# Drawing the waits on two PSUM tensors by bank instead of by tensor

## The chip, the cores and the metric

The kernel runs on one core of a Trainium2 chip. The metric is the device time of one execution in microseconds (us). The core has five engines that run their own instruction streams and meet through semaphores: PE (TensorE, matrix products), DVE (VectorE), ACT (ScalarE), POOL (GpSimd) and SP (here the queue that issues most DMAs). PE writes its products into PSUM, a memory of eight banks; DVE and ACT read them from there.

## The reference, cut to what matters

```python
# q, k, v: 8 batches x 8 heads x 576 positions x 64
scores = q @ k.T / 8                       # heads 0-3: the last 32 positions;
attn = softmax(where(mask, scores, -1e9))  # heads 4-7: same position modulo 32, not later
x = (attn @ v)                             # as 4608 tokens x 512
h = x @ w_in                               # 4608 x 1024
e = exp(h - max(h)); sm = e / (sum(e) + 1e-9)
solu = h * sm
ln = (solu - mean(solu)) / sqrt(var(solu) + 1e-6) * g_ln
out = ln @ w_out                           # 4608 x 512
```

## The kernel before

The work has two halves that run side by side. The attention is cut into 40 units, five for each of the 8 batches. A unit's scores are made by PE in the PSUM tensor `s_ps` (L445 puts the mask in, L450 adds the products). DVE takes the maxima (L456) and subtracts them (L457), ACT takes the exponential (L459), DVE, POOL and ACT normalise it, a DMA turns it (`pt`, L480), and PE multiplies it by v into `x_ps` (L502). ACT (L518) and DVE (L519) copy the result as a high and a low f16 part into `xhi` and `xlo`.

The feed-forward part is cut into 36 tiles of 128 tokens, numbered 0 to 35 here; function `ff(n, ...)` writes tile n. For one tile:

1. PE makes the first product (`x @ w_in`) into two banks of `h_ps`, in two halves of 512 columns. A half is 12 products of 512 columns (L560, L561, L562 in turn).
2. DVE takes the negated maximum of both halves (L567) and prepares scales (L568, L574, L575).
3. ACT takes the exponential out of `h_ps` (L578, into `eu`; each such instruction is followed by a short row that reads the accumulated sum).
4. DVE multiplies `h_ps` by that exponential (L581, into `eu` too) and makes a mean (L584). It is the last reader of the tile's two banks.
5. ACT and DVE make the f16 parts `c` (L585, L586), ACT the squares (L588), POOL the norm's factor (L592 to L596), and a DMA turns `c` into `ct` (L599).
6. PE makes the second product (L604, L605, L606) into `o_ps`, also in two halves of 12. ACT scales it (L612) and issues the store (L613).

The PSUM tensors are `s_ps` (2 banks), `h_ps` (3), `x_ps` (2) and `o_ps` (1). In the last tiles (34 and 35) the second product goes to `s_ps`, and tile 35's first product to `x_ps`. A tile's first product uses two of the three banks of `h_ps`: banks 0 and 1, then 0 and 2, then 1 and 2, in a cycle of three tiles; the half that is made first goes to the bank that the tile just before does not use.

Class `Plan` collects all steps (`add`) with an engine, an estimated time, a key, and what each step reads and writes, by bank for `h_ps` and `x_ps` (names such as `("h", 1)`, `("x", 0)`). `order` makes one list of all steps from the keys and these dependencies, and the kernel then calls every step's function in that order. Each engine executes its instructions in that order, one after the other. The waits between engines are not drawn from the plan: the layer under the kernel draws them while the instructions are recorded, from the tensors that each instruction reads and writes. For a PSUM tensor it puts an access of one engine behind the accesses of other engines that were recorded before it, whichever bank of the tensor they touch. If the plan's list has the first half of tile n+1 ahead of the exponential of tile n, that exponential therefore waits for that half, although it lies in another bank.

A per-batch scale is also made: ACT sums squares of v (L378), DVE adds two of them up (L325), PE spreads the sum over the partitions (L332, into `s_ps`), and DVE makes the scale (L336 to L342). w_out is prepared early, by ACT and DVE (L629 to L631, L685, L686).

Of the kernel before, what the change touches and what calls it, by code (L numbers as in the profile page):

```python
# [86 lines left out]
]  # L87


class Plan:  # L90

# [6 lines left out]
    SKIP = {"act": 0.1, "dve": 0.08, "pe": 0.07, "pool": -0.1}  # L98

    def __init__(self):  # L100
        self.steps = []
        self.writer, self.readers = {}, {}

    def add(self, eng, dur, fn, key, r=(), w=(), lock=None, dma=None, after=()):

        n = len(self.steps)
        deps = set(after)
        for x in r:
            if x in self.writer:
                deps.add(self.writer[x])  # L110
        for x in w:
            if x in self.writer:
                deps.add(self.writer[x])
            deps.update(self.readers.get(x, ()))
        for x in r:
            self.readers.setdefault(x, []).append(n)
        for x in w:
            self.writer[x], self.readers[x] = n, []
        deps.discard(n)
        lock = eng == "pool" if lock is None else lock  # L120
        self.steps.append((eng, dur, fn, key, deps, lock, dma))
        return n

    def order(self):
        steps = self.steps
        left = [len(s[4]) for s in steps]
        users = [[] for _ in steps]
        for n, s in enumerate(steps):
            for d in s[4]:
                users[d].append(n)  # L130
        ready_at = [0.0] * len(steps)
        free = dict.fromkeys(("pe", "act", "dve", "pool", "sp"), 0.85)
        locked = dict.fromkeys(("dve", "pool"), 0.0)
        dma_free, moved, pieces = 3.0, 0, []
        waiting = {e: [] for e in free}
        for n, s in enumerate(steps):
            if not left[n]:
                waiting[s[0]].append(n)
        out = []
        while len(out) < len(steps):  # L140
            best = None
            for e, ns in waiting.items():
                if not ns:
                    continue
                now = max(free[e], min(ready_at[n] for n in ns))
                n = min((n for n in ns if ready_at[n] <= now), key=lambda n: (steps[n][3], n))
                if best is None or now < best[0]:
                    best = now, e, n
            now, e, n = best
            waiting[e].remove(n)  # L150
            out.append(n)
            dur = steps[n][1]
            if e == "sp":
                pushes, issue, begins, lands = steps[n][6]
                start = max(now + begins, dma_free)
                dma_free = start + dur
                pieces.append((start, dma_free, moved, moved + pushes))
                moved += pushes
                free[e] = now + issue + 0.06
                for a, b, c, d in reversed(pieces):  # L160
                    if c < moved - self.DEEP <= d:
                        free[e] = max(free[e], a + (b - a) * (moved - self.DEEP - c) / (d - c))
                        break
                end = dma_free + lands + (LATE0 if steps[n][6] == LOAD and now < 20 else self.LATE)
            else:
                if steps[n][5]:
                    now = max(now, locked["pool" if e == "dve" else "dve"])
                    locked[e] = now + dur
                end = now + dur
                free[e] = end - (0.16 if dur > 2.4 else self.SKIP[e])  # L170
            for m in users[n]:
                left[m] -= 1
                ready_at[m] = max(ready_at[m], end + (0.0 if steps[m][0] == e else self.HOP))
                if not left[m]:
                    waiting[steps[m][0]].append(m)
        self.span = max(free.values())
        return out


@with_exitstack  # L180
def attn_solu_kernel(ctx: ExitStack, tc: tile.TileContext, qloc, qstr, kloc, kstr, vloc, vstr, w_in, w_out, g, masks, out):
    nc = tc.nc
# [63 lines left out]
    h_ps = ps.tile([P, 3, 512], F32, name="h_ps")  # L246
    x_ps = ps.tile([P, 2, 512], F32, name="x_ps")
    o_ps = ps.tile([P, DM], F32, name="o_ps")

    plan = Plan()  # L250
# [3 lines left out]
    def init():  # L254
        for i, x in enumerate((-0.5, DEEP * P_SCALE / TOP, P_SCALE)):
            nc.gpsimd.memset(consts[:, i : i + 1], x)
        for x in vsc_sb:
            nc.gpsimd.memset(x[:, 3:4], 1.0 / TOP)
            nc.gpsimd.memset(x[:, 4:5], -1.0 / TOP)

    add("pool", 1.2, init, -9, w=["consts"])
    add("dve", 0.3, lambda: nc.vector.memset(ones, 1.0), -9, w=["ones"])

    def masks_bf16():
# [6 lines left out]
    def load_masks(key):  # L271
        add("sp", 0.4, lambda: nc.sync.dma_start(mask_sb, masks), key, w=["mask_raw"], dma=LOAD)
        add("dve", 1.0, masks_bf16, key, r=["mask_raw"], w=["mask"])
# [248 lines left out]

    def ff(n, key, key2):

        banks, halves = (((0, 1), (0, 1)), ((0, 2), (1, 0)), ((1, 2), (0, 1)))[n % 3]
        hv, o, O = h_ps[:, banks[0] : banks[1] + 1 : banks[1] - banks[0]], o_ps, "o"
        HH = [("h", i) for i in banks]

        if n >= NT - 2:
            o, O = s_ps[:, n % 2], ("s", n % 2)  # L530
        if n == NT - 1:
            hv, HH = x_ps, [("x", i) for i in range(2)]
# [7 lines left out]
        nm, up, down, low, z, us, mean, sq, near, ia, zb, zc, v, r, f = (st[:, i : i + 1] for i in range(15))  # L540
# [23 lines left out]
        for i in halves:  # L564
# [4 lines left out]
            r=[(ST, "low"), *SC, "consts"], w=[(ST, "nm")])  # L569

        def span():
# [7 lines left out]
            r=[*HH, (ST, "nm"), *SC], w=[E, (ST, "z")])  # L579

        add("dve", 1.3, lambda: nc.vector.scalar_tensor_tensor(uv, hv, ia, ev, op0=ALU.mult, op1=ALU.mult, accum_out=us), key + 0.3,  # L581
            r=[*HH, E, (ST, "ia")], w=[U, (ST, "us")])
# [4 lines left out]
            r=[U, (ST, "mean"), (C, 0)], w=[(C, 1)], lock=True)  # L587
        add("act", 1.24, lambda: nc.scalar.activation(junk[:, 0:DF], u, AF.Square, bias=mean, scale=1.0, accum_out=sq), key + 0.42,  # L588
            r=[U, (ST, "mean")], w=["junk", (ST, "sq")])
# [109 lines left out]
    for b in range(B):  # L699
        if b:  # L700
            load_qk(b, 1, LK[b])
        v_split(b, 1, VK[b] + 0.5)
        for j in range(2):
            unit(b * NU + j, UK[b * NU + j], PK[b * NU + j])
        if b:
            load_qk(b, 0, LK[b] + 2)
        v_split(b, 0, VK[b] + 2.5)
        for j in range(2, NU - 1):
            unit(b * NU + j, UK[b * NU + j], PK[b * NU + j])
        if b + 1 < B:  # L710
            if b == 0:
                prep_o()
            load_v(b + 1, 1, LK[b + 1] + 0.5)
            load_v(b + 1, 0, LK[b + 1] + 2.5)
            v_scale(b + 1, VK[b + 1])
        unit(b * NU + NU - 1, UK[b * NU + NU - 1], PK[b * NU + NU - 1])
        if b == 0:
            split_o()
        while t < NT and (t * P + P - 1) // S <= b:
            ff(t, TK[t], GK[t])  # L720
            t += 1

    for n in plan.order():
        plan.steps[n][2]()


# [59 lines left out]
```

## Time and profile before

| | before |
|---|---|
| median of 3 runs | 530.99 us (529.46 to 534.56) |
| the profiled execution | 528.67 us, of it a span of 527.0 us from the first to the last instruction |
| mean granted TensorE clock | 0.974 |
| PE busy | 476.0 us (90%) |
| DVE busy | 359.3 us (68%) |
| ACT busy | 294.3 us (56%) |
| POOL busy | 153.8 us (29%) |

In a view of groups or of waits a row names the engine, the tensor written and the line. "A <- B: 5.7, 7, 1.4" says that A's engine sat idle before it for 5.7 us in total, in 7 waits of which the longest was 1.4 us, and that B ended those waits. In a timeline a row is: start, duration, engine, line, operation, out<-in with shapes, how many in a row, and in brackets the idle time of the engine just before it with what ended it. A step that waited although its engine was busy with nothing shows this idle time; products of 512 columns start about 0.22 us apart and have rows of 0.38 us, since they overlap in the array.

### The profile page before, as it was taken

The numbers are of one execution on the slowest core, as the hardware profiler recorded it, in microseconds if no ns is written. First come the engines' busy times: TensorE is split into PE (matmuls) and PEld (weight loads), VectorE is DVE, ScalarE is ACT, GpSimd is POOL, SyncE is SP. The second block draws the span as 40 slices with busy tenths as digits, with TensorE's granted clock in tenths as the row PEclk, the third lists the DMA queues.
The fourth block names the chain that finished last, engine by engine and source line by source line (L and its number), as shares of the span: only waits on it lengthen the run. The fifth ranks groups of instructions, "written<-read, shape, count | busy, mean of one in ns | idle before, by whom it ended". The sixth has DMA issues, their size and how long they took to land.

```text
span 527.0 us, 11895 instructions
## 1 busy us (share of the span) xinstructions
PE 476.0 (90%) x4858; PEld 246.1 (47%) x4858; DVE 359.3 (68%) x679; ACT 294.3 (56%) x414; POOL 153.8 (29%) x258
## 2 busy tenths in 40 slices
PE   1547969989999999989999899999998999989996
PEld 1434534444544555445544455545543545444442
DVE  3597978577964888477954878577963789743540
ACT  1689966574736555645646456735655546433441
POOL 4342562423421233223331242212331223211120
PEclk9857998999999999999999999999999999999999
DMA  8999998449996799839995499989973597723351
GB/s 231 406 320 267 313 262 177 91 106 223 243 207 131 165 241 227 176 95 194 309 182 108 117 202 298 196 201 228 221 132 69 144 199 143 121 62 82 78 107 54
DMA packets 168294, 96.51 MB, mean 183 GB/s; under 512 B 138032, under 2 KB 154800, under 8 KB 167728
## 3 DMA queue, kind: packets, MB, share of 16 engines
q1 hardware_dynamic: 163056, 86.32, 75.3%
q10 hardware_dynamic: 5184, 9.44, 5.6%
q8 instruction: 38, 0.62, 0.5%
q14 instruction: 16, 0.13, 0.1%
HBM read 40.03 MB, written 9.44 MB: 94 GB/s over the span
## 4 chain that ended last, share of the span: by engine, by line
PE 74%; DVE 12%; DMA 5%; issue 4%; ACT 3%; POOL 1%; SPq 0%; ACTq 0%; DVEq 0%; POOLq 0%
PE h_ps L560 12%; PE h_ps L562 11%; PE h_ps L561 11%; PE o_ps L604 9%; PE o_ps L605 8%; PE o_ps L606 8%; PE s_ps L450 4%; PE x_ps L502 4%; DVE st L567 3%; DVE eu L581 3%; DMA vtwo<-vstr 2%; DMA pt<-p 2%; PE s_ps L445 1%; PE h_ps L656 1%; DMA ct<-c 1%
## 5 line engine op out<-in xcount | busy, mean ns | idle before, releaser
L560 PE MATMUL h_ps<-w,xhi 128*128 128x512 f16 x280 | 107.0, 382 | 8.8 <-DVE eu L581 5.7
L561 PE MATMUL h_ps<-w,xhi 128*128 128x512 f16 x280 | 106.9, 382 | 0.0
L562 PE MATMUL h_ps<-w,xlo 128*128 128x512 f16 x280 | 106.7, 381 | 0.1
L604 PE MATMUL o_ps<-obuf,ct 128*128 128x512 f16 x272 | 103.4, 380 | 0.9 <-ACT ob L612 0.8
L606 PE MATMUL o_ps<-obuf,ct 128*128 128x512 f16 x272 | 103.1, 379 | 0.0
L605 PE MATMUL o_ps<-obuf,ct 128*128 128x512 f16 x272 | 103.1, 379 | 0.0
L468 POOL TENSOR_TENSOR t<-t,m 128x576 f32<-128x576 f32 (+2 forms) x40 | 52.3, 1309 | 135.8 <-DVE m L465 106.1
L581 DVE SCALAR_TENSOR_TENSOR eu<-h_ps,st,eu 128x1024 f32<-128x1024 f32 x35 | 44.8, 1280 | 40.7 <-PE h_ps L562 19.2
L567 DVE TENSOR_REDUCE st<-h_ps 128x1 f32<-128x1024 f32 x35 | 42.6, 1218 | 42.3 <-PE h_ps L562 42.0
L585 ACT ACTIVATE c<-eu,st 128x1024 f16<-128x1024 f32 x36 | 41.3, 1147 | 41.2 <-DVE st L584 39.5
L578 ACT ACTIVATE eu<-h_ps,st,vsc 128x1024 f32<-128x1024 f32 x31 | 37.3, 1204 | 47.8 <-DVE st L568 22.1
L586 DVE SCALAR_TENSOR_TENSOR c<-eu,st,c 128x1024 f16<-128x1024 f32 x36 | 45.9, 1276 | 22.1 <-ACT c L585 22.1
L594 POOL TENSOR_SCALAR st<-st 128x1 f32<-128x1 f32 x36 | 23.5, 653 | 120.9 <-ACT junk L588 120.0
L561 PEld LDWEIGHTS <-xhi 128*128 128x128 f16 x288 | 28.3, 98 | 41.0 <-issue 11.2
L459 ACT ACTIVATE t<-t 128x576 f32<-128x576 f32 (+2 forms) x40 | 27.5, 686 | 33.9 <-DVE t L457 32.6
L562 PEld LDWEIGHTS <-xlo 128*128 128x128 f16 x288 | 28.3, 98 | 34.9 <-issue 0.8
L604 PEld LDWEIGHTS <-ct 128*128 128x128 f16 x288 | 28.1, 97 | 34.7 <-issue 3.1
L606 PEld LDWEIGHTS <-ct 128*128 128x128 f16 x288 | 28.2, 98 | 34.0
L560 PEld LDWEIGHTS <-xhi 128*128 128x128 f16 x288 | 28.3, 98 | 32.7 <-issue 0.8
L450 PE MATMUL s_ps<-k,q 64*54 64x54 f32 (+1 forms) x1280 | 41.1, 270 | 2.7 <-DMA k<-kstr 1.8
L605 PEld LDWEIGHTS <-ct 128*128 128x128 f16 x288 | 28.2, 98 | 31.7 <-issue 2.2
L450 PEld LDWEIGHTS s_ps<-k,q 64*54 64x54 f32 (+1 forms) x1280 | 39.5, 198 | 3.3 <-issue 3.3
(148 smaller groups left out, 704.9 us busy)
## 6 DMA issues: line engine op xcount, KB each, us to landing
out<-ob ACTq DMA_DIRECT2D x36, 256.0 KB, 3.3
vtwo<-vstr SPq DMA_DIRECT2D x9, 768.0 KB, 7.2
vd<-vtwo SPq DMA_DIRECT2D x14, 384.0 KB, 9.0
vrl<-vloc SPq DMA_DIRECT2D x8, 640.0 KB, 5.7
q<-qstr SPq DMA_DIRECT2D x8, 594.0 KB, 4.9
k<-kstr SPq DMA_DIRECT2D x8, 594.0 KB, 5.6
q<-qloc SPq DMA_DIRECT2D x8, 576.0 KB, 4.5
k<-kloc SPq DMA_DIRECT2D x8, 576.0 KB, 6.8
```

The costliest lines, as they stand in the source:

```text
L450: nc.tensor.matmul(s_ps[row : row + nq, pair, i * nk : (i + 1) * nk], q_raw[half][hs, q0 : q0 + (nq - 1) * nqb + 1 : nqb], k_raw[half][hs, ...
L468: add("pool", nx * nk / 510 + 0.02, lambda: nc.gpsimd.tensor_tensor(tv, tv, sm.unsqueeze(2).broadcast_to([P, nx, nk]), op=ALU.mult), key + ...
L560: nc.tensor.matmul(hv[:, i], xhi[:, cc, tok], whi[:, cc, cols], start=(cc == 0), stop=False)
L561: nc.tensor.matmul(hv[:, i], xhi[:, cc, tok], wlo[:, cc, cols], start=False, stop=False)
L562: nc.tensor.matmul(hv[:, i], xlo[:, cc, tok], whi[:, cc, cols], start=False, stop=(cc == 3))
L567: add("dve", 1.21, lambda: nc.vector.tensor_reduce(low, hv, axis=AX.XY, op=ALU.max, negate=True), key + 0.2, r=HH, w=[(ST, "low")])
L581: add("dve", 1.3, lambda: nc.vector.scalar_tensor_tensor(uv, hv, ia, ev, op0=ALU.mult, op1=ALU.mult, accum_out=us), key + 0.3, r=[*HH, E, ...
L585: add("act", 1.2, lambda: nc.scalar.activation(c[:, 0], u, AF.Identity, bias=mean, scale=1.0), key + 0.35, r=[U, (ST, "mean")], w=[(C, 0)])
L586: add("dve", 1.28, lambda: nc.vector.scalar_tensor_tensor(c[:, 1], u, mean, c[:, 0], op0=ALU.add, op1=ALU.subtract), key + 0.4, r=[U, (ST, ...
L604: nc.tensor.matmul(o, ct[:, cc, :], ohi[:, cc, :], start=(cc == 0), stop=False)
L605: nc.tensor.matmul(o, ct[:, cc, :], olo[:, cc, :], start=False, stop=False)
L606: nc.tensor.matmul(o, ct[:, 8 + cc, :], ohi[:, cc, :], start=False, stop=(cc == 7))
```

## The change

A step's PSUM waits on `h_ps` and `x_ps` are taken out of the hands of the layer below and drawn from the plan's dependencies. `Plan.add` notes for each PE, ACT and DVE step which of the two tensors it touches. A new function `emit` replaces the loop that called the steps. After a step is recorded, it declares that its instructions do not depend on another engine's earlier accesses to the same tensor, except on those of the steps that the plan names; and it adds, for each of these, a wait of the step's first instruction for the last instruction of the named step. On PE a step's first instruction is a weight load, so a wait that stood at the product can now stand at the weight load ahead of it.

The banks of a tile change too: even tiles use banks 0 and 1, odd tiles banks 1 and 2, and odd tiles make their second half of columns first. So the first half made goes to bank 0 or 2, which the tile before last used, and the second half made always goes to bank 1, which the tile just before uses.

```diff
+BANKED = ("h", "x")
...
     def add(self, eng, dur, fn, key, r=(), w=(), lock=None, dma=None, after=()):
...
+        self.spaces.append({x[0] for x in (*r, *w) if isinstance(x, tuple) and x[0] in BANKED} if eng in ("pe", "act", "dve") else set())
         self.steps.append((eng, dur, fn, key, deps, lock, dma))
...
+def emit(nc, tc, plan):
+    same_bank = mybir.DependencyInfo(mybir.DependencyClass.Sync, mybir.DependencyReason.DATA)
+    made = {}
+    for n in plan.order():
+        eng = plan.steps[n][0]
+        k = len(nc.cur_bb.bb.instructions)
+        plan.steps[n][2]()
+        if not plan.spaces[n]:
+            continue
+        made[n] = new = list(nc.cur_bb.bb.instructions[k:])
+        for x in sorted(plan.spaces[n]):
+            true = [d for d in sorted(plan.steps[n][4]) if x in plan.spaces[d] and plan.steps[d][0] != eng]
+            for i in new:
+                for other in ("pe", "act", "dve"):
+                    if other != eng:
+                        tc.declare_no_dep(i, group=x + other, keep=[j for d in true for j in made[d]], reason="another bank")
+            for d in true:
+                tc.add_manual_dep(new[0], made[d][-1].name, same_bank, reason="the same bank")
+        for x in sorted(plan.spaces[n]):
+            for i in new:
+                tc.add_to_no_dep_group(x + eng, i)
...
     def ff(n, key, key2):
-        banks, halves = (((0, 1), (0, 1)), ((0, 2), (1, 0)), ((1, 2), (0, 1)))[n % 3]
-        hv, o, O = h_ps[:, banks[0] : banks[1] + 1 : banks[1] - banks[0]], o_ps, "o"
+        banks, halves = (((0, 1), (0, 1)), ((1, 2), (1, 0)))[n % 2]
+        hv, o, O = h_ps[:, banks[0] : banks[1] + 1], o_ps, "o"
...
-    for n in plan.order():
-        plan.steps[n][2]()
+    emit(nc, tc, plan)
```

The new function pushes the lines below it down by 28, so that the first product stands at L588 to L590 after the change. No instruction changes its place on any engine: all five lists are the same, line numbers apart. What moves are the waits. In the rows below the names in brackets are the semaphores for which an instruction waits, each named after the engine that raises it.

The first place is on PE, where the first half of tile 28's first product (into `h_ps`, from `xhi` and `xlo`) follows the end of a second product (`o_ps`). Before:

```order
L606 LDWEIGHTS ct_107
L606 MATMUL o_ps<-obuf_121,ct_107 128x512
L560 LDWEIGHTS xhi_101 [waits Activation_49]
L560 MATMUL h_ps<-w_120,xhi_101 128x512 [waits Activation_49]
L561 LDWEIGHTS xhi_101
L561 MATMUL h_ps<-w_120,xhi_101 128x512
```

After:

```order
L634 LDWEIGHTS ct_107
L634 MATMUL o_ps<-obuf_121,ct_107 128x512
L588 LDWEIGHTS xhi_101 [waits Activation_49]
L588 MATMUL h_ps<-w_120,xhi_101 128x512
L589 LDWEIGHTS xhi_101
L589 MATMUL h_ps<-w_120,xhi_101 128x512
```

The wait at the product, which was for tile 27's exponential (L578 on ACT), is gone; the wait at the weight load, for the copy into `xhi` (L518), stays.

The second place is on DVE, from the maximum of tile 31 (L567, `st_115`) to the start of tile 32's. Before:

```order
L567 TENSOR_REDUCE st_115<-h_ps 128x1 [waits PE_49]
L568 TENSOR_TENSOR st_115<-st_115 128x3 [waits DVE_49]
L574 TENSOR_SCALAR st_115<-st_115 128x1 [waits DVE_49]
L575 TENSOR_SCALAR st_115<-st_115 128x1 [waits DVE_49]
L581 SCALAR_TENSOR_TENSOR eu_104,st_115<-h_ps,st_115,eu_104 128x1024 [waits DVE_49,PE_49,Activation_49]
L584 TENSOR_SCALAR st_115<-st_115 128x1 [waits DVE_49]
```

After:

```order
L595 TENSOR_REDUCE st_115<-h_ps 128x1 [waits PE_49]
L596 TENSOR_TENSOR st_115<-st_115 128x3 [waits DVE_49]
L602 TENSOR_SCALAR st_115<-st_115 128x1 [waits DVE_49]
L603 TENSOR_SCALAR st_115<-st_115 128x1 [waits DVE_49]
L609 SCALAR_TENSOR_TENSOR eu_104,st_115<-h_ps,st_115,eu_104 128x1024 [waits DVE_49,Activation_49]
L612 TENSOR_SCALAR st_115<-st_115 128x1 [waits DVE_49]
```

The multiplication of tile 31 (L581) no longer waits for PE: that wait was for the first half of tile 32. In many other places, such as the maxima (L567) of tiles 13 and 18, the brackets read the same before and after, but the count that is waited for is lower: it was that of the next tile's first half, which is recorded earlier, and is now that of the tile's own second half.

Of the 72 halves, 22 have a wait at the first weight load before and 44 after; the first product itself has one in 44 before and in none after.

More of the change, by code (lines that the diff above doesn't have):

```diff
@@ L100, in __init__ @@
     def __init__(self):
-        self.steps = []
+        self.steps, self.spaces = [], []
         self.writer, self.readers = {}, {}
```

## The prediction

> **What bounds the kernel now.** I read the page first, for the engine that is never free.
>
> ```profile
> span 527.0 us, 11895 instructions
> PE 476.0 (90%) x4858; PEld 246.1 (47%) x4858; DVE 359.3 (68%) x679; ACT 294.3 (56%) x414; POOL 153.8 (29%) x258
> PE   1547969989999999989999899999998999989996
> L560 PE MATMUL h_ps<-w,xhi 128*128 128x512 f16 x280 | 107.0, 382 | 8.8 <-DVE eu L581 5.7
> ```
>
> PE is busy for 476.0 of 527.0 us. So a wait is worth what it leaves PE idle, and no more: 51 us in all. The row of 40 slices (13.2 us each, busy tenths) shows where: much of it lies in the first four slices, where the weights are prepared, and from the seventh on PE is at 8 or 9 tenths until the last. The view of waits says which can be touched by this change.
>
> ```profile
> DVE eu L581 <- PE h_ps L562: 19.2, 6, 4.7
> ACT eu L578 <- PE h_ps L562: 14.1, 5, 4.1
> PE s_ps L445 <- DVE t L457: 5.9, 3, 5.0
> PE h_ps L560 <- DVE eu L581: 5.7, 7, 1.4
> PE s_ps L332 <- DVE vs L325: 4.4, 4, 1.5
> PE x_ps L502 <- DVE xlo L519: 3.2, 1, 3.2
> PE h_ps L560 <- ACT eu L578: 1.9, 2, 1.6
> PE h_ps L560 <- DVE st L567: 0.8, 2, 0.4
> ```
>
> The first two rows are DVE and ACT waiting, for 33.3 us, for a first product that is not their own tile's (their own is done when L567 has read it). DVE and ACT have time to spare, so these 33 us count only where PE then waits for DVE or ACT. That is what the six rows of PE show.
>
> **The change part by part.** No instruction is added, removed or moved, so the sum is one of PE's idle times that go.
>
> *First halves that wait for another bank.* Tile 28's is the largest.
>
> ```profile
> 405.36 1.18 ACT L578 ACTIVATE eu<-h_ps,st,vsc 128x1024 f32<-128x1024 f32 x1
> 406.69 0.38 PE L560 MATMUL h_ps<-w,xhi 128*128 128x512 f16 x1 [1.58 <-ACT eu L578]
> 406.90 0.38 PE L561 MATMUL h_ps<-w,xhi 128*128 128x512 f16 x1
> ```
>
> PE sits idle for 1.58 us until tile 27's exponential (406.54) and its read-out are over. That exponential reads banks 0 and 1; the half goes to bank 2. The order's rows show that the wait goes. Its bank's last reader, by the new numbering bank 0, was tile 26.
>
> *Second halves that wait for a late multiplication.* The second half shares its bank with the tile just before, before and after the change, and must wait for that tile's L581. But L581 was itself held.
>
> ```profile
> 466.08 0.19 ACT L578 ACTIVATION_READ_ACCUMULATOR eu<-h_ps,st 128x1 f32 x1
> 470.06 1.28 DVE L581 SCALAR_TENSOR_TENSOR eu<-h_ps,st,eu 128x1024 f32<-128x1024 f32 x1 [4.68 <-PE h_ps L562]
> 471.41 0.38 PE L560 MATMUL h_ps<-w,xhi 128*128 128x512 f16 x1 [1.44 <-DVE eu L581]
> ```
>
> Tile 31's exponential is there at 466.27. DVE idles 4.68 us until PE has finished tile 32's first half (just under 470), multiplies until 471.4, and PE idles 1.44 us for it. With the false wait gone the multiplication ends near 467.7, before PE asks.
>
> Not every such wait is false. At 68.45 DVE comes to L581 without any idle time (its row has no bracket), so this wait stays:
>
> ```profile
> 67.11 1.28 DVE L581 SCALAR_TENSOR_TENSOR eu<-h_ps,st,eu 128x1024 f32<-128x1024 f32 x1
> 68.45 0.38 PE L560 MATMUL h_ps<-w,xhi 128*128 128x512 f16 x1 [1.23 <-DVE eu L581]
> 79.92 0.56 PE L560 MATMUL h_ps<-w,xhi 128*128 128x512 f16 x1 [0.21 <-DVE eu L581]
> ```
>
> I keep 68.45 and 79.92 (1.4 us). The three rows of L560 add up to 5.7 + 1.9 + 0.8 = 8.4 us, so **7.0 us** go, in 9 waits.
>
> *The scale of v, L332.* L325 stands behind a maximum (L567) on DVE, and that maximum waits for the next tile's first half.
>
> ```profile
> 223.98 0.38 PE L562 MATMUL h_ps<-w,xlo 128*128 128x512 f16 x1
> 223.99 0.19 ACT L378 ACTIVATION_READ_ACCUMULATOR junk<-vtwo 128x1 f32 x1
> 226.98 1.23 DVE L567 TENSOR_REDUCE st<-h_ps 128x1 f32<-128x1024 f32 x1 [6.58 <-PE h_ps L562]
> 228.32 0.16 PE L332 MATMUL s_ps<-vs,ones 128*128 128x1 bf16 x1 [1.38 <-DVE vs L325]
> 341.10 0.16 PE L332 MATMUL s_ps<-vs,ones 128*128 128x1 bf16 x1 [0.22 <-DVE vs L325]
> ```
>
> Tile 13's product ends with the row at 223.98 (224.4), its maximum starts 2.6 us later, and L325's other input is ready at 224.18. Started at 224.4, the maximum and L325 are done before 226; PE asks at 226.9. Of the 4.4 us in four waits, the one at 341.10 (0.22 us) has no such maximum ahead of it and stays; the other two are built like this one: **4.2 us** go.
>
> *The copies of x, L502 at 78.72.* Here too a maximum holds DVE.
>
> ```profile
> 70.82 0.38 PE L562 MATMUL h_ps<-w,xlo 128*128 128x512 f16 x1
> 74.62 1.23 DVE L567 TENSOR_REDUCE st<-h_ps 128x1 f32<-128x1024 f32 x1 [2.40 <-PE h_ps L562]
> 78.12 0.55 DVE L519 TENSOR_TENSOR xlo<-x_ps,xhi 128x384 f16<-128x384 f32 x1
> 78.72 0.99 PE L502 MATMUL x_ps<-pt,vd 118*64 118x54 f16 x48 [3.22 <-DVE xlo L519]
> ```
>
> DVE's 2.40 us go (it waits for tile 2's first half; its own product was done at 71.2, with the row at 70.82), everything between on DVE follows, and PE's 3.22 us shrink by **2.4 us**.
>
> *The clock behind that wait.* Two windows after it (PE's busy time and count come first, the granted clock third from the end):
>
> ```profile
> 79.90:83.50 3.60, 3.58 (x9) 1.31 (x9) 3.60 (x7) 3.52 (x6) 0.00 (x0) 0.53 0.92 181
> 83.50:87.00 3.50, 3.50 (x18) 1.56 (x16) 3.50 (x5) 2.09 (x4) 1.23 (x1) 1.00 1.10 248
> ```
>
> After 3.22 us idle the granted clock is 0.53 for 3.6 us: 9 products where the next 3.5 us hold 18. That costs half of it, 1.8 us. A wait of 1.58 us (tile 28's) was followed by products at full distance, 0.21 us. With 0.8 us left at this place I expect no dip: **1.8 us**; the other end is 0, if the dip stays. The Trainium skill ("TensorE: Matmul & The Clock Gate", Part 1) says that the clock halves after an idle window of about 3.4 us, which runs freely. The trace agrees in size (0.53, 3.6 us). By that rule the dip's going would be likely and not certain, and the sum would stay within these two ends.
>
> *The mask's product, L445.* Of the three waits for L457 (5.9 us) the longest, 5.0 us, is in the preparation; the other two, 0.9 us, come late, the first of them here:
>
> ```profile
> 422.60 1.28 DVE L581 SCALAR_TENSOR_TENSOR eu<-h_ps,st,eu 128x1024 f32<-128x1024 f32 x1 [2.70 <-PE h_ps L562]
> 425.56 0.31 PE L445 MATMUL s_ps<-mk_str,unit 64*64 64x270 bf16 x4 [0.48 <-DVE t L457]
> ```
>
> DVE comes to these L457 without idle time after a false wait of 2.70 us: **0.9 us** go.
>
> *What the idle figures leave out.* The rows at 406.69 and 406.90 start 0.21 us apart but last 0.38, so a stall behind a 512-column product is longer than its idle figure by 0.17 us. Nine of the waits above stand behind such a product: **1.5 us**.
>
> *The waits that move to the weight load.* These could cost. A half's weights take 98 ns to load, and 44 halves now carry a wait there, 22 more than before. Exposed each time that is 22 x 0.1 = 2.2 us; where the wait is long satisfied it may be nothing. Tile 7's first half has its wait at the weight load already:
>
> ```profile
> L560 PEld LDWEIGHTS <-xhi 128*128 128x128 f16 x288 | 28.3, 98 | 32.7 <-issue 0.8
> 142.57 0.38 PE L606 MATMUL o_ps<-obuf,ct 128*128 128x512 f16 x1
> 142.79 0.38 PE L560 MATMUL h_ps<-w,xhi 128*128 128x512 f16 x1
> ```
>
> It starts 0.22 us after the product ahead, the full rate. I take 0, and keep 2.2 for the range. The Trainium skill (same page, Part 2, step 1) says that PE pulls weight loads ahead of products in flight. That speaks against the change, since a load that waits can't be pulled ahead; by it the sum would be 15.6 us. The row above shows no such loss.
>
> **Sum:** 7.0 + 4.2 + 2.4 + 1.8 + 0.9 + 1.5 = 17.8 us.
>
> *What is late next.* PE then reaches its other waits earlier. One is already tight:
>
> ```profile
> 92.22 1.28 DVE L581 SCALAR_TENSOR_TENSOR eu<-h_ps,st,eu 128x1024 f32<-128x1024 f32 x1 [0.48 <-ACT eu L578]
> 93.60 0.39 PE L560 MATMUL h_ps<-w,xhi 128*128 128x512 f16 x1
> 75.00:100.00 25.00, 21.57 (x222) 10.65 (x215) 21.70 (x41) 15.50 (x24) 10.41 (x14) 0.93 0.74 166
> ```
>
> L581 ended at 93.5. Mostly these follow PE's own earlier work and move with it; where DVE has little room (21.70 of 25 us here) they do not. Between nothing and all given back, I am nearer to nothing, because every DVE and ACT wait that goes lets them run ahead as well: 3.8 us, a fifth. **Net 14.0 us.** The profiled execution took 528.67 us, 1.67 around its span, and would take 514.7. The median of the runs is 530.99, 2.3 above it; taken off that, **517.0 us**.
>
> The last stretch does not help or hurt: PE's waits there are for ACT's L612 reading `o_ps` and `s_ps`, which the change leaves alone.
>
> **The rivals.**
>
> *Next waits take the place* (most of the gain is lost). If DVE's dense stretches, 25 to 100 us, and the attention's waits (L445 for L457) bind, PE's removed idle time comes back as another. For it: the tight wait at 93.60. Against it: DVE is 68% busy, and some 33 us of its and ACT's own waiting go. What surely stays are the direct first halves, 1.9 + 0.8 = 2.7 us, and about half of the rest: (17.8 - 2.7) / 2 + 2.7 would be 10; at a quarter it is 6.5 us, so 524.5 us.
>
> *The change doesn't do what it says.* Where the layer below still orders `h_ps` by tensor through another semaphore, the time stays at 531. Against it are the order's rows at tiles 28 and 31.
>
> *Slower, by DMAs that land later.* All turned tiles go through one queue. If the earlier starts of `ct` and `pt` fall together with loads, each lands later, and PE meets it. None of PE's waits above ended on a DMA, so the room is unknown. To eat up 17.8 us, the 36 `ct` would have to reach PE 0.5 us late each; at 0.7 us the kernel is at 538. Nothing points to it: a transfer that starts earlier has as much longer to land.
>
> **How the numbers follow.** Forecast (10 to 18 us gained, 513 to 521): 0.62. More than that, since ACT and DVE may also hurry the early stretch: 0.05. The next waits: 0.25, centred at 524.5, of which 0.18 lies below 525.7. Without effect: 0.05. Slower: 0.03. Faster by over 1% (below 525.7; 1% is about what a measurement of this kernel can tell from no change) is then 0.62 + 0.05 + 0.18 = 0.85; within 1% 0.07 + 0.05 = 0.12; slower 0.03. The range leaves out 2 in 10: from 511.5 (all of the sum and 1.7 us more) to 525, which takes in the dip of the clock, the 2.2 us of weight loads and most of the first rival.
>
> **What the profile will show.** Right: the rows of DVE's and ACT's waits for `h_ps` products of another tile (19.2 and 14.1 us) are gone or small; L588's idle time (now 8.8) falls to about 2; the four waits of L332 keep under 1 us; the granted clock has no dip near 78 us; PE's busy time hardly changes, since the rows are the same. Wrong would be: L588's idle time at 8 again, L473 or L530 (the mask's and x's products) with several us of new idle time, or products spaced wider than 0.22 us.

## The result and the profile after

The changed kernel takes 514.18 us (median, 512.16 to 520.89) against 530.23 us (529.14 to 534.56) of the kernel before in the same session: a ratio of 0.967, 95% interval 0.959 to 0.975. The forecast was 517.0 us with a range of 511.5 to 525. An execution over 1.5% above the fastest of its kernel is not in a ratio: 520.89 us here, and in the second measurement of the changed kernel further down 526.30 and 702.49 us of its six (and 821.70 us of the kernel before).

The profiled execution took 512.16 us, of it a span of 510.4: 16.6 us less than the span before. First the page: the span, the engines, PE's row of slices, and three groups.

```profile
span 510.4 us, 11874 instructions
PE 474.6 (93%) x4858; PEld 246.3 (48%) x4858; DVE 360.0 (71%) x679; ACT 296.0 (58%) x414; POOL 154.6 (30%) x258
PE   1548989999999999999999999999999999999996
L588 PE MATMUL h_ps<-w,xhi 128*128 128x512 f16 x280 | 107.2, 383 | 1.5 <-DVE eu L609 1.4
L606 ACT ACTIVATE eu<-h_ps,st,vsc 128x1024 f32<-128x1024 f32 x31 | 37.3, 1203 | 33.8 <-DVE st L596 33.4
L609 DVE SCALAR_TENSOR_TENSOR eu<-h_ps,st,eu 128x1024 f32<-128x1024 f32 x35 | 44.7, 1277 | 8.2 <-ACT eu L606 7.9
```

PE does the same work (474.6 us busy against 476.0), and from the seventh slice on every slice but the last stands at 9. L588's idle time fell from 8.8 to 1.5 us. The exponential and the multiplication now wait for what they use, and no longer for PE: the view of waits has no row any more in which one of them waits for a product. Of its rows these bear on the forecast:

```profile
DVE st L595 <- PE h_ps L590: 43.5, 23, 4.2
PE s_ps L473 <- DVE t L485: 5.0, 1, 5.0
PE x_ps L530 <- DMA pt<-p: 2.6, 2, 1.5
PE h_ps L588 <- DVE eu L609: 1.4, 2, 1.2
PE s_ps L360 <- DVE vs L353: 0.2, 1, 0.2
```

The first row is DVE's wait for its own tile (42.0 us before, when some of it was for the next tile's half: the longest was 6.8 us, now 4.2). Of the waits of PE that the sum named, the two that were to stay stayed (L588, 1.2 and 0.2 us), and so did the one in the preparation (L473, 5.0). One row is longer than before: the transposed weights of the attention, `pt` (1.9 us in one wait before, now two).

Four places of the timeline, in time order:

```profile
152.10 0.82 PE L530 MATMUL x_ps<-pt,vd 118*64 118x54 f16 x40 [1.16 <-DMA pt<-p]
393.72 1.20 ACT L606 ACTIVATE eu<-h_ps,st,vsc 128x1024 f32<-128x1024 f32 x1 [0.86 <-DVE st L596]
394.60 0.38 PE L588 MATMUL h_ps<-w,xhi 128*128 128x512 f16 x1
455.35 0.38 PE L588 MATMUL h_ps<-w,xhi 128*128 128x512 f16 x1
```

Tile 28's first half starts at 394.60 without idle time, while tile 27's exponential is still running (393.72 to 394.92): they are on different banks, and that is the change at work. Tile 31's second half (455.35) finds its bank free. The row at 152.10 is the one new wait.

### The profile page after: what moved, and what is told of

Same layout as the page of the kernel before. It is cut to its first block, busy times and chain, and to the rows that moved or that the text cites. A ratio compares the mean times of both kernels' runs of the same rounds, so it can differ in the third digit from the quotient of the medians.

```text
span 510.4 us, 11874 instructions
## 1 busy us (share of the span) xinstructions
PE 474.6 (93%) x4858; PEld 246.3 (48%) x4858; DVE 360.0 (71%) x679; ACT 296.0 (58%) x414; POOL 154.6 (30%) x258
## 4 chain that ended last, share of the span: by engine, by line
PE 81%; DMA 6%; DVE 5%; ACT 2%; issue 2%; SPq 2%; POOL 1%; ACTq 0%; POOLq 0%
PE h_ps L588 11%; PE h_ps L589 11%; PE h_ps L590 11%; PE o_ps L632 11%; PE o_ps L634 10%; PE o_ps L633 10%; PE s_ps L478 6%; PE x_ps L530 5%; DMA k<-kloc 4%; DMA pt<-p 3%; PE s_ps L473 2%; DVE obuf L714 1%; PE h_ps L684 1%; DVE eu L609 1%; SPq L448 1%
## 5 line engine op out<-in xcount | busy, mean ns | idle before, releaser
L588 PE MATMUL h_ps<-w,xhi 128*128 128x512 f16 x280 | 107.2, 383 | 1.5 <-DVE eu L609 1.4
L590 PE MATMUL h_ps<-w,xlo 128*128 128x512 f16 x280 | 106.7, 381 | 0.0
L632 PE MATMUL o_ps<-obuf,ct 128*128 128x512 f16 x272 | 103.4, 380 | 0.9 <-ACT ob L640 0.8
L595 DVE TENSOR_REDUCE st<-h_ps 128x1 f32<-128x1024 f32 x35 | 42.7, 1220 | 43.5 <-PE h_ps L590 43.5
L622 POOL TENSOR_SCALAR st<-st 128x1 f32<-128x1 f32 x36 | 21.4, 595 | 108.6 <-ACT junk L616 107.6
L546 ACT CAST xhi<-x_ps 128x384 f16<-128x384 f32 (+2 forms) x40 | 21.7, 547 | 41.5 <-PE x_ps L530 36.6
L484 DVE TENSOR_REDUCE m<-s_ps 128x6 f32<-128x576 f32 (+2 forms) x40 | 30.4, 760 | 21.2 <-PE s_ps L478 21.2
L590 PEld LDWEIGHTS <-xlo 128*128 128x128 f16 x288 | 28.4, 98 | 34.4 <-issue 0.8
L588 PEld LDWEIGHTS <-xhi 128*128 128x128 f16 x288 | 28.2, 98 | 34.5 <-DVE eu L609 1.9
L632 PEld LDWEIGHTS <-ct 128*128 128x128 f16 x288 | 28.1, 98 | 31.7
```

Of the source, the lines that this page charges most:

```text
L588: nc.tensor.matmul(hv[:, i], xhi[:, cc, tok], whi[:, cc, cols], start=(cc == 0), stop=False)
L590: nc.tensor.matmul(hv[:, i], xlo[:, cc, tok], whi[:, cc, cols], start=False, stop=(cc == 3))
L595: add("dve", 1.21, lambda: nc.vector.tensor_reduce(low, hv, axis=AX.XY, op=ALU.max, negate=True), key + 0.2, r=HH, w=[(ST, "low")])
L632: nc.tensor.matmul(o, ct[:, cc, :], ohi[:, cc, :], start=(cc == 0), stop=False)
```

## Where the 16.5 us came from

PE's instruction list is the same, so the same half of a first product can be looked up in both timelines, and the difference of its starts is the time gained so far:

| start before | start after | gained | what lies between this row and the one above |
|---|---|---|---|
| 53.31 | 53.15 | 0.16 | the preparation |
| 71.82 | 73.36 | -1.54 | after: the clock is halved from 68.9 to 72.3 |
| 79.92 | 78.39 | 1.53 | the wait of L502 at 78.72 |
| 84.19 | 80.99 | 3.20 | before: the clock is halved from 80.0 to 83.4 |
| 115.37 | 110.52 | 4.85 | L332's first wait (1.5), a short one of L560 (0.3), less 0.15 at the tight place (93.60 before, 90.55 after) |
| 154.91 | 148.18 | 6.73 | three waits of L560 |
| 164.47 | 158.98 | 5.49 | after: the wait for `pt` at 152.10 |
| 232.72 | 225.23 | 7.49 | a wait of L560, L332's second wait |
| 296.15 | 287.10 | 9.05 | L332's third wait |
| 399.77 | 389.40 | 10.36 | two waits of L560 (1.1), a short one inside a half (0.3) |
| 406.69 | 394.60 | 12.09 | tile 28's first half (1.58 + 0.17) |
| 430.97 | 417.65 | 13.32 | the two late waits of L445 (1.0), a short one of L560 (0.1) |
| 458.08 | 443.63 | 14.46 | L560 |
| 471.41 | 455.35 | 16.06 | tile 31's wait (1.44 + 0.17) |
| 477.06 | 460.53 | 16.53 | the last wait of L560 |

It stays at 16.53 to the last first product. Added up by kind, as the sum of the prediction has them (its 1.5 us for what the idle rows leave out is shared among the nine waits that it was for: five of L560, two of L332, two of L445):

| | forecast | found |
|---|---|---|
| L560's waits | 7.0 + 0.9 | 8.8 |
| L332 | 4.2 + 0.3 | 4.6 |
| L502 | 2.4 | 3.1 |
| L445 | 0.9 + 0.3 | 1.0 |
| smaller steps | - | 0.4 |
| the clock | 1.8 | 0.0 |
| what is late next | -3.8 | -1.4 |
| net | 14.0 | 16.5 |

## The experiments

All kernels below are the changed kernel with the edit shown; none changes the work of PE, DVE or ACT, and where the output changes it is said. Ratios are to the kernel before on the same chip.

**Which part of the change?** The first edit keeps the new banks and leaves all waits to the layer below:

```diff
-BANKED = ("h", "x")
+BANKED = ()
```

> The new banks of the tiles alone, with all waits drawn by tensor as before. Theory (the gain is the removed waits, and the renumbering of banks only makes them removable): the time of the kernel before, ratio 1.00, about 530 us, with PE's 8.4 us of idle time ahead of L588 back. Rival (contiguous banks let the layer below tell banks apart by itself): 514 to 518 us, and PE's idle time ahead of L588 under 3 us.

Measured: 531.38 us, 0.997 (0.994 to 1.001). The waits are those of before, to the tenth:

```profile
DVE eu L609 <- PE h_ps L590: 19.2, 6, 4.7
ACT eu L606 <- PE h_ps L590: 14.1, 5, 4.1
PE h_ps L588 <- DVE eu L609: 5.7, 7, 1.4
```

The two-tile alternation of banks is worth nothing by itself. The other half of that question, waits by bank with the old cycle of three, was not tried: a tile on banks 0 and 2 is read by one access that steps over bank 1, while PE may be writing there. The next two name one tensor each:

```diff
-BANKED = ("h", "x")
+BANKED = ("h",)
```

> Waits by bank for h_ps alone, x_ps by tensor. Theory (nearly all of it comes from h_ps; of the waits named in the prediction none was a false one on x_ps): 514 to 516 us, ratio 0.970. Rival (the copies L546 and L547, freed of each other, carry much of it): 519 us or more, ratio 0.98 or above.

Measured: 514.31 us, 0.966 (0.959 to 0.972): the whole gain.

```diff
-BANKED = ("h", "x")
+BANKED = ("x",)
```

> Only the attention's output (x_ps) is drawn by bank, h_ps as in the kernel before. Theory that the whole gain is of h_ps: 1.000 of before (531 us), the exponentials' wait for h_ps and the idle 8.8 us at L588 as before. Rival, x_ps has a share of its own: 0.995 or less, with the waits of xhi and xlo for TensorE shorter.

Measured: 530.29 us, 1.000 (0.997 to 1.002), with the multiplication's 19.2 us of waits for products as before. So all of it that the times can tell is `h_ps`.

**Whose waits?** The waits of `h_ps` stand on both sides: PE waits for readers of the other bank, and the readers (DVE, ACT) wait for PE's products in the other bank. The next two free one side each, in `emit`:

```diff
-                    if other != eng:
+                    if other != eng and eng == "pe":
```

> PE's instructions are freed of other banks' readers; DVE and ACT still wait for products recorded earlier, whichever bank. Theory: only the first halves that waited themselves gain: 1.9 + 0.8 + 0.97 (tile 31's first half, held by tile 30's multiplication) = 3.7 us of idle time, with 0.17 us more for each of five waits 4.5 us, so ratio 0.991, about 526 us. Rival (PE's own waits were the larger part): 520 us or less.

Measured: 527.11 us, 0.992 (0.987 to 0.996), as expected. In the page (its execution, 531.79 us, is the longest of the ten):

```profile
L588 PE MATMUL h_ps<-w,xhi 128*128 128x512 f16 x280 | 107.8, 385 | 5.3 <-DVE eu L609 4.8
```

and in the waits:

```profile
DVE eu L609 <- PE h_ps L590: 18.6, 6, 4.7
PE s_ps L360 <- DVE vs L353: 4.4, 4, 1.5
```

PE's direct waits go (3.5 us of L588's idle time), the readers' stay, and with them L360 and L588's second halves.

```diff
-                    if other != eng:
+                    if other != eng and eng != "pe":
```

> DVE and ACT are freed of other banks' products; PE still waits for other banks' readers. Theory: the rest of the 16.6 us, some 12 us: late multiplications, the four L360 and the copies at 78.72; ratio 0.977, about 518 us, with PE's idle time ahead of L588 at 4 to 5 us. Rival (readers' waits are covered, since DVE and ACT have time to spare): 526 us or more.

Measured: 514.42 us, 0.966 (0.959 to 0.973): not the 0.977 that was expected; the times can't tell it from the changed kernel. Tile 28's half still waits for tile 27's exponential by the program, but that exponential is no longer late itself. In the page:

```profile
L588 PE MATMUL h_ps<-w,xhi 128*128 128x512 f16 x280 | 106.4, 380 | 3.9 <-DVE eu L609 2.8
```

and tile 28's half in the timeline:

```profile
395.28 0.38 PE L588 MATMUL h_ps<-w,xhi 128*128 128x512 f16 x1 [0.31 <-ACT eu L606]
```

Of 1.58 us 0.31 are left. L588's idle time falls from 8.8 us by 3.5 with PE freed, by 4.9 with the readers freed, and by 7.3 with both: less than the two together. The waits of the two sides are links of one loop (PE waits for a reader that waits for PE), and opening it at either place frees part of the same time. The expectation had added the sides up as if they were apart. The 2.4 us that are left on L588 are half a per cent, below what these runs tell.

**Does a wait in the middle come back one for one at the end?** Here only the maxima (L595) of tiles 4, 13 and 18 wait for the whole tensor again. They are what made L325 (now L353) late.

```diff
-                    if other != eng:
+                    if other != eng and n not in plan.held:
...
+        if n in (4, 13, 18):
+            plan.held.add(low_n)
```

> Only the maxima of tiles 4, 13 and 18 wait for the whole tensor again, as in the kernel before; all else as changed. Theory that a wait of TensorE in the middle of the program comes back one for one at the end: the three transposes of L360 wait 1.45, 1.38 and 1.38 us again, with 0.17 us that an idle row leaves out for each, 4.7 us in all, so 1.009 of the changed kernel (about 519 us on a median of 514). Rival, cover: the order has slack behind these places (the same work waits elsewhere anyway), then 1.000. Rival, knock-on: what stands behind the late maxima makes TensorE wait again, then 1.015 or more, with new idle rows at L588 or L632.

It ran beside the changed program itself, which was measured once more for this:

> The changed program once more, to give the next three kernels their base on one chip. All theories: 0.967 of before (514 us), no maximum and no exponential of a first product's tile waits for TensorE longer than its own product, L588 idle below 2 us.

Measured: the changed kernel 0.9685 (0.963 to 0.974), with the three held maxima 0.9802 (0.976 to 0.985), 521.02 us: 1.012 of the changed kernel, where 1.009 was expected and the uncertainty of each ratio is half a per cent. The three waits of L360 are back in their old size:

```profile
108.51 0.16 PE L360 MATMUL s_ps<-vs,ones 128*128 128x1 bf16 x1 [1.46 <-DVE vs L353]
224.84 0.16 PE L360 MATMUL s_ps<-vs,ones 128*128 128x1 bf16 x1 [1.38 <-DVE vs L353]
289.02 0.16 PE L360 MATMUL s_ps<-vs,ones 128*128 128x1 bf16 x1 [1.38 <-DVE vs L353]
337.60 0.16 PE L360 MATMUL s_ps<-vs,ones 128*128 128x1 bf16 x1 [0.22 <-DVE vs L353]
```

At each of the first three PE loses 1.5 us against the changed kernel, 4.6 us together (4.7 were expected). So the waits came back at the end, and the rival by which the order covers them (1.000) is out. The time alone doesn't tell 1.009 from the knock-on's 1.015, but the rows do: L588 waits for the multiplication for 1.4 us, as in the changed kernel, and the only other waits of PE over 0.3 us from 85 us on are one for `pt` (1.76 us at 145.56) and the two at the end. A wait on DVE, off the busiest engine, thus costs what it leaves PE idle two steps later.

**What is late next: `pt`.** The new wait at 152.10 has a transposing transfer behind it that stood on the SP queue behind three copies of v. From the queue's timeline of the changed kernel:

```profile
132.66 6.26 SPq L508 DMA_TRANSPOSE pt<-p  x1
139.03 3.01 SPq L627 DMA_TRANSPOSE ct<-c  x1
142.13 0.54 SPq L393 DMA_DIRECT2D vrl<-vloc  x1
142.77 3.73 SPq L448 DMA_DIRECT2D ve<-vl  x3
146.61 1.38 SPq L508 DMA_TRANSPOSE pt<-p  x1
```

The waits for `pt` are not the same in every execution of one program. The second profile of the changed kernel, of an execution that took 526.30 us, has three long ones:

```profile
134.62 0.28 PE L530 MATMUL x_ps<-pt,ve 96*64 96x64 f16 x6 [1.34 <-DMA pt<-p]
150.06 1.44 PE L530 MATMUL x_ps<-pt,vd 118*64 118x54 f16 x48 [3.20 <-DMA pt<-p]
208.88 1.49 PE L530 MATMUL x_ps<-pt,vd 118*64 118x54 f16 x48 [2.99 <-DMA pt<-p]
```

Behind the second the clock is halved for a window (after the window's length PE's busy time comes first, and the granted clock stands third from the end):

```profile
146.74:150.15 3.41, 0.21 (x7) 0.20 (x8) 1.81 (x4) 0.00 (x0) 0.00 (x0) 1.00 1.23 224
150.15:153.56 3.41, 3.41 (x54) 1.98 (x54) 1.29 (x2) 2.02 (x3) 0.00 (x0) 0.50 1.06 248
```

Before the tests of the place on the queue, a change at the end that they carry too. PE's two last waits, 0.82 us each at 490.01 and 503.95, are of L632 for ACT's copy L640. With `s_ps` drawn by bank as well, and tile 33's second product in the third bank of `h_ps`, neither has to wait:

```diff
-BANKED = ("h", "x")
+BANKED = ("h", "x", "s")
...
+        if n == NT - 3:
+            o, O = h_ps[:, 2], ("h", 2)
```

> The third PSUM tensor is drawn by bank too, and the second product of tile 33 goes to the third bank of h_ps, so that no two last second products share a bank with a copy that is late. Theory: the two waits of L632 near the end (0.82 us each, with 0.17 us more that an idle row leaves out) go, 2.0 us, so 0.996 of the changed kernel. Rival: the end hangs on the copies and the output's transfer, then 1.000.

Measured: 514.77 us, 0.969 (0.964 to 0.974), no difference from the changed kernel that the times could tell. In the profile the two waits are gone, and from the last three of the first products (L588 to L590) to the end of PE's work it is 21.53 us instead of 23.50: the 2.0 us are there, and were lost in the same execution to other waits for `pt` (2.91 us at 201.44). The next kernel also puts three copies of v behind the transpose that follows them on the SP queue:

```diff
+    rest = [n for n in order[: at + 1] if n not in plan.late]
+    for n in [*rest, *plan.late, *order[at + 1 :]]:
...
+            if (b, a) == (1, 0):
+                plan.late.append(moved)
```

> As the one before, and on the SP queue the three ve copies of the first batch's first half stand behind the next transposing transfer of p instead of ahead of it. Theory that the wait at L530 near 152 us (1.16 us, new in the changed kernel) comes from that transfer standing 3.73 us behind the three copies: it goes, another 1.2 to 1.3 us, so 0.993 to 0.994 of the changed kernel. Rival: the transfer lands late anyway, by the time that it takes, or the ve copies are now late for the value products: no better than the one before, or slower, with the wait still at L530.

Measured: 515.83 us, 0.969 (0.964 to 0.973). The wait stayed, but the edit had missed its place: it moved the copies near 84 us, and the ones that were meant are still ahead of the transfer.

```profile
145.98 3.91 SPq L453 DMA_DIRECT2D ve<-vl  x3
155.16 0.82 PE L537 MATMUL x_ps<-pt,vd 118*64 118x54 f16 x40 [1.11 <-DMA pt<-p]
```

It says nothing on the queue. With `(b, a) == (2, 0)` the right copies move:

> Like e8, but with the copies that were meant there: e8 moved those that stand near 79 us (the second batch's), and the transposing transfer for which TensorE waits near 152 us kept the three ve copies of the third batch ahead of it. Here these stand behind it, so that it is issued 3.7 us earlier. Theory of the queue (the transfer is late because of its place): no wait at L530 for pt between 148 and 157 us, and at most the one near 142 to 145 us stays. Rival, the load (the transfer crawls because the loads' bytes are on the DMA engines): a wait of about 1 us stays there. In time, 0.997 or more of e7 for both, too little to tell from it.

Measured: 512.79 us, 0.966 (0.962 to 0.971), again not to be told from the changed kernel, so no version here is shown to beat it. PE has no wait for `pt` of over 0.1 us between 43 and 270 us, but one of 2.53 us at 271.91.

```profile
144.44 2.37 SPq L515 DMA_TRANSPOSE pt<-p  x1
146.86 2.45 SPq L453 DMA_DIRECT2D ve<-vl  x3
149.43 1.57 SPq L515 DMA_TRANSPOSE pt<-p  x1
```

The other side is the load. Here the loads of q, k and v are left out from the third batch on (that batch and the later ones compute with what the second left, so the output is another):

```diff
-nc.sync.dma_start(vr_sb[a], (vloc, vstr)[a][b])
+b > 1 or nc.sync.dma_start(vr_sb[a], (vloc, vstr)[a][b])
```

(and the same for q and k)

> As changed, with the loads of q, k and v of the batches from the third on left out (the third batch on then reads what the second left; the copies within the chip stay). Theory that the late transposes of p between 130 and 156 us (TensorE waits 0.5 to 4.5 us for them in each profile so far that has TensorE early there) are late because these loads' bytes are on the DMA engines with them: no wait at L530 for pt there, 0.963 to 0.965 of before. Rival, the transposes' own length and their turn on the SP queue: the wait stays, 0.967.

Measured: 512.80 us, 0.968 (0.965 to 0.972). PE waits for no `pt` after 43 us, although the copies stand where they stood. On the queue:

```profile
131.42 1.51 SPq L508 DMA_TRANSPOSE pt<-p  x1
135.21 1.73 SPq L627 DMA_TRANSPOSE ct<-c  x1
139.29 2.47 SPq L448 DMA_DIRECT2D ve<-vl  x3
141.87 5.14 SPq L508 DMA_TRANSPOSE pt<-p  x2
```

The transpose that held SP for 6.26 us is issued in 1.51. In time it is no gain that these runs can tell (0.963 to 0.965 was expected): in this execution the wait at L338 near 66 us was longer (1.42 us against 0.82) and the clock stayed halved for two windows there. Without the copies of v too, from the second batch on (the output changes here too):

> As the one before, with the copies of the split values into ve and vd left out as well from the second batch on, so that the SP queue holds nothing but transposes from there. Theory of the loads: no better than the one before. Rival, the copies: only here is the wait for pt gone, 0.963 to 0.965. Second rival, the transposes alone: it stays even here.

Measured: 511.38 us, 0.965 (0.963 to 0.967), no wait for `pt` after 43 us either. The four executions lie within 510.75 to 511.96 us, where the four of the changed kernel that count in its second measurement, on another chip, lay within 511.80 to 516.65.

So the late `pt` goes with the loads, as far as ten profiles tell. The eight in which PE runs early with the loads in place all have waits for `pt` after 48 us, 1.2 to 3.3 us in total and 7.5 us in the execution of 526.30 us; the two without loads have none. From 100 us on, the slowest `pt` took 9.3 us from issue to landing in the changed kernel, and 6.8 and 5.8 us without the loads. What the place on the queue does is not shown: the waits stand at other places in each profile, and the kernel with the new end alone, its loads and copies where they were, has no wait for `pt` between 133 and 201 us either. One profile without the wait near 152 therefore proves nothing. What exactly slows a transpose next to a load was not tried.

## Why the prediction was right

**The mechanism held step by step.** The waits named went where the sum said: L588 keeps 1.5 us (about 2 was expected), L360 0.2 of 4.4, L473 loses its two late waits, PE's busy time is the same. The terms of the waits, 16.0 us, came out at 17.5. The surplus is L560's and L502's. Of L560, three waits of 0.12 us or less, which the view of waits doesn't list, brought 0.7 us together. That 0.17 us goes with each idle row behind a 512-column product is borne out by tile 28, which gained 1.73 us for an idle row of 1.58.

L502 only looks sized low (3.1 for 2.4). In the profile of the kernel with only the readers freed, in which the clock is not halved here, the wait is

```profile
75.95 0.99 PE L530 MATMUL x_ps<-pt,vd 118*64 118x54 f16 x48 [0.76 <-DVE xlo L547]
```

so 2.5 us have gone and 0.8 are left, as forecast. In the changed kernel the halved clock from 68.9 on delays PE, DVE's work that doesn't need PE runs on, and 0.15 us of the wait is left: some 0.6 us of what that dip cost came back here.

**Weight loads.** The 44 waits there cost nothing: outside the waits in the table, PE's two last ones (L632) and the halved clock, no product behind a 512-column product starts over 0.12 us later than its 0.22. From 60 us on, the halved clock aside, PE loses over 0.05 us against the kernel before in two places only: at the wait for `pt`, and 0.15 us at the tight place. The bound of 2.2 us is not seen, nor the sum of 15.6 us that was worked out for loads that can't be pulled ahead.

**The step that failed most is "what is late next"**: 3.8 us were taken off, 1.4 were lost. The tight place at 93.60 cost 0.15 us and no more, because the readers move ahead with PE. What binds is a transfer, which the prediction had among its rivals only with 18 us and more. It argued there that none of the waits of PE that it had listed ended on a DMA; the same view had this row (the wait is at 42.24, in the preparation), which the list left out:

```profile
PE x_ps L502 <- DMA pt<-p: 1.9, 1, 1.9
```

The waits for `pt` reached 3.3 us, and 7.5 in one execution, so the direction of that rival was right and its price too high.

**Where it was luck.** The gains were forecast at 17.8 us and come to 17.9, but 1.8 of the forecast were the clock, which brought nothing, and the waits brought 1.9 more. The two large misses, the clock and what is late next, pull in opposite directions (1.8 too much, 2.4 too little), which brings the net nearer to the forecast than its parts are.

**The clock's 1.8 us did not come**, and the reason given for it was incomplete. The windows, before and after (columns as above):

```profile
66.30:69.74 3.44, 1.92 (x14) 1.09 (x15) 3.19 (x9) 1.28 (x3) 2.35 (x2) 1.00 1.57 147
76.57:79.98 3.41, 1.05 (x49) 1.04 (x49) 3.38 (x7) 3.41 (x7) 2.92 (x3) 1.00 1.36 279
79.98:83.39 3.41, 3.41 (x9) 1.23 (x9) 3.41 (x7) 3.33 (x6) 0.00 (x0) 0.50 0.93 183
```

```profile
65.52:68.93 3.41, 1.36 (x13) 0.77 (x12) 3.41 (x7) 1.23 (x3) 2.66 (x2) 1.00 1.66 177
68.93:72.34 3.41, 3.41 (x9) 1.22 (x8) 2.67 (x8) 2.85 (x4) 1.67 (x2) 0.50 0.78 230
```

The stretch at half clock (a dip) behind the removed wait is gone, as forecast. But another stands at 68.9, behind two waits that both kernels have (0.82 us at L310, now L338, and 1.24 at the kept L588). The half-clock stretches of a profile begin at whole multiples of 3.41 us from one another (17.0 and 14.0 of them here, counted from the stretch in the preparation), and the windows above lie on that grid. In the window from 65.52 PE is idle for 3.41 - 1.36 = 2.05 us, and the next window is at half clock. Before, the same two waits were cut by a window's edge: from 66.30 on PE is idle for 1.5 us, and no dip follows. Where the edge falls differs from execution to execution, so this is chance, and here it fell the other way. The profile of the kernel with only the readers freed, with the window at another place again:

```profile
65.73:69.14 3.41, 1.65 (x13) 0.96 (x14) 3.38 (x9) 1.40 (x4) 2.60 (x2) 1.00 1.73 161
69.14:72.55 3.41, 3.41 (x51) 1.84 (x49) 3.05 (x7) 3.41 (x5) 1.73 (x1) 1.00 0.84 253
```

Here 1.76 us of idle time are followed by a full clock. Over the fourteen profiles of this case, from 48 us on, and for windows whose next one lies within the span: all 16 windows at full clock with 2.0 us of idle time or more were followed by half clock, none of those with 1.58 or less was, and of the six between (1.64 to 1.76) three were. Where PE has work throughout, a dip costs half a window: 1.7 us at 80.0 before and 1.7 us at 68.9 after.

The Trainium skill ("TensorE: Matmul & The Clock Gate", Part 1) puts the window at 3413 ns and says that it runs freely; the grid of 3.41 us agrees. It lets the clock fall after an idle window; here a window that was idle for 2.0 of its 3.41 us was enough, and the measurement decides.

## What to carry to other kernels

Where several banks of PSUM are one tensor, look for engines that wait for an instruction on another bank: here 33 us of such waits on DVE and ACT, which are not the busiest engines, stood behind most of PE's idle time after the first 60 us (20.0 us before, 5.6 after). Price them by the idle time of the bounding engine and add what its idle rows leave out. Do not add up the two sides of a loop of waits: freeing the readers alone brought all of the gain that the times could tell. Take little off for "what is late next" where the engines that are waited for are freed by the same change, and look for it on the transfers.

## What the runs showed of the hardware that was not expected

- The granted clock was halved for a window of 3.41 us whenever PE had been idle for 2.0 us or more of the window before, in one piece or in two (16 of 16); with 1.58 us or less it never was, and between 1.64 and 1.76 us in three of six. Waits that come to some 2 us can so cost 1.7 us more in one execution and not in the next, by where the window's edge falls.
- The same transposing transfers are late at other places in each execution (0.1 to 4.5 us of PE's time between 130 and 160 us in the profiles with PE early and the loads in place). With the loads and copies left out, four executions lay within 1.2 us, where four of the changed kernel on another chip lay within 5; so this and the clock behind it are probably a large part of the spread, which is not shown.
